# Layer-2 weight conversion, weight sums and pair operands moved from GpSimd to VectorE, and all first-layer casts to ScalarE, in a spectral MLP kernel

## The chip, the core and the metric

The kernel runs on one core of a Trainium2 chip. Its engines are TensorE (PE, matrix products; PEld is its weight load), VectorE (DVE), ScalarE (ACT), GpSimd (POOL) and SyncE (SP), which issues DMAs. The metric is the device time of one execution in microseconds; a kernel's time is the median of several runs.

## What is computed

```python
X = rfft(x, axis=1)                                  # x: (2, 3008, 256)
Yr = Xr @ w_r - Xi @ w_i + b_r;  Yi = Xr @ w_i + Xi @ w_r + b_i
Y = soft-threshold of both by 0.01
x = irfft(Y).reshape(6016, 256)
h = x @ w_in1;  g = max(h, 0) + alpha * min(h, 0);   x = g @ w_out1    # layer 1, 2048 wide
h = x @ w_in2;  g = h if h >= 1, 0 if h <= -1, else (h + 1)**2 / 4     # layer 2, 2048 wide
out = g @ w_out2
```

Every product of the two layers is made of three matmuls: each operand is split into a high part in fp32r (a rounding cast, `gh`, `mxh`, `xo[0]`) and a low part (the fp32 value less its high part, `gl`, `mxl`, `xo[1]`), and low x high, high x low and high x high are added up in PSUM.

## The kernel before

**Stages.** A Fourier stage fills the first 190 us or so. Layer 1 works on 12 chunks of columns, five of 512 and one of 448 for each of the two batches, and 16 blocks `f` of 128 hidden units: 192 steps. The first three chunks are interleaved ("the trio"), and the other nine follow one after the other. One step is `first` (6 matmuls into `psh`, then `ta` and `tb` on ScalarE, a scalar_tensor_tensor on VectorE that joins them into `ta`, then the split of `ta` into `gh` and `gl`) and `second` of the step three back (6 matmuls from `gh`, `gl` into `pso`). `ta` and `tb` have two buffers each, `gh` and `gl` four, `psh` two to four banks. So `ta` of a step waits until `gl` of the step two back has been taken out of the same buffer.

Layer 2 works on six column groups ("pairs", four of 2 x 512 columns and two of 2 x 480) with 8 `quad`s each, 48 in all. A quad makes a 2 x 2 block product from 7 products M1 to M7 in place of 8; it needs sums of the weights (`sum_weights`, three closures for each of the 8 quads of a pair) and sums of the inputs (`prep_pair`, eight stages for each pair). Its 24 output matmuls (`pq`) come one quad later, in four groups.

**Order.** The order of every engine's queue is that in which the code is written; nothing reorders it. Work that isn't part of the step is put in by generators and lists of closures: `conv` (the weight conversion from 64-bit words, pieces of it taken by `next(conv)`), `jobs` and `events`.

**What the change touches.** In the trio, the cast `gh <- ta` is on ScalarE and is written one step later, behind `ta` and `tb` of the next step (`split_late`); in chunks 3 to 11 it is on VectorE at once (`late_split`, L462 to L492). The conversion of layer 1's weights has `conversions(0, ..., V)` and is cut into four pieces for each weight; that of layer 2's weights has `conversions(1, order1, G)`, two pieces for each weight, and its clamp (L194), product (L176), low part (L182) and sum (L183) are on GpSimd. So are the sums L602 to L616 and the differences L643 to L665 of `sum_weights` and `prep_pair`; their high parts (L615, L642) are ScalarE casts. The first pair's operands and the first three weight sums are made during layer 1, are written to DRAM (`keep`) and come back near its end (`fetch`).

Of the kernel before, what the change touches and what calls it, by code (L numbers as in the profile page):

```python
# [89 lines left out]
def spectral_mlp_kernel(ctx: ExitStack, tc: tile.TileContext, x, w_r, w_i, bias, c_f1, c_f2,  # L90
# [483 lines left out]
    X_TAGS = ["c1", "w5", "w6", "w7", "w8", "w9", "w10", "p5", "c2", "c3"]  # L574
    S_TAGS = ["w4", "w11", "w12", "w0", "w1", "w2", "p3", "p4"]
# [17 lines left out]
    def sum_weights(l, j):  # L593
# [3 lines left out]
        def whole():  # L597
            t = block("p0" if j < 3 else "c0", [128, 2, 512], F32, f"sfr{l}_{j}")
            held.extend((t[:, 0, :], t[:, 1, :]))
            for i in range(2):  # L600
                w = wt[l, 2 * j + i]
                G.tensor_tensor(held[0][:, 256 * i:256 * i + 256], w[:, 0, 0:256].bitcast(F32),  # L602
                                w[:, 1, 0:256].bitcast(F32), op=ALU.add)

        def add():
            f4, r4 = (t.rearrange("p (k m) -> p k m", k=4) for t in held)
            G.tensor_tensor(r4[:, 0], f4[:, 2], f4[:, 3], op=ALU.add)
            G.tensor_tensor(r4[:, 2], f4[:, 0], f4[:, 2], op=ALU.subtract)
# [12 lines left out]

        return whole, add, cut

    def prep_pair(p):
# [3 lines left out]
        held = []  # L628
# [4 lines left out]
        def operand(name, v):  # L633
# [130 lines left out]
    def quad(l, p, j, prev, extra, last=False):  # L764
# [21 lines left out]
        A.activation(s5, ps["C"], AF.Copy)  # L786
        if prev:
# [58 lines left out]
    def fetch_w15():  # L846
        wt[1, 15] = fetch(10, "w3", "w1_15k")
# [4 lines left out]
    def fetch_x(k):  # L852
# [3 lines left out]
    ahead = {1: [lambda: fetch_x(0)], 4: [fetch_w15], 5: [lambda: fetch_s(0)], 12: [lambda: fetch_s(1)],  # L856
             13: [lambda: fetch_s(2)]} | {5 + k: [lambda k=k: fetch_x(k)] for k in range(1, 7)}
# [87 lines left out]
```

## Time and profile before

| | us |
|---|---|
| median of 3 runs | 1140.19 (1139.62 to 1140.55) |
| profiled execution | 1139.39 |
| its span from the first to the last instruction | 1137.5 |
| PE busy | 1115.3 (98%) |
| DVE busy | 944.4 (83%) |
| ACT busy | 725.2 (64%) |
| POOL busy | 224.9 (20%) |

Busy time of PE alone does not tell whether it runs at its pace: its matmuls are pipelined, each is shown longer than the distance to the next, so a PE that starts its matmuls late can still look busy. The pace is read from the distance between starts, or from the time that a step or a quad takes. The granted clock is 1.00 in nearly every stretch, which is the upper one of its two levels.

### The profile page before, as it was taken

The page shows a single profiled execution, that of the slowest core. Times are in us where ns is not written, and L with a number is a line of the kernel's source. Part 1 is how long each engine was busy: PE and PEld are TensorE (multiplying, and loading weights), DVE is VectorE, ACT ScalarE, POOL GpSimd, SP SyncE. Part 2 cuts the span into 40 slices and gives each one's busy share as a digit, 9 for nine tenths or more (in the row PEclk, how much of TensorE's full clock was granted, in tenths as well). Part 3 has the DMA queues.
Part 4 walks back from the last instruction along what each step waited for, and adds up shares of the span by engine and source line. Part 5 has one row for each costly group of instructions (what it writes and reads, how often), then busy time and mean ns, then how long its engine had stood idle before and what let it go on. Part 6 is the DMA issues. An engine that isn't in the chain of part 4 may idle for free.

```text
span 1137.5 us, 17421 instructions
## 1 busy us (share of the span) xinstructions
PE 1115.3 (98%) x6488; PEld 983.2 (86%) x6488; DVE 944.4 (83%) x1446; ACT 725.2 (64%) x1356; POOL 224.9 (20%) x190
## 2 busy tenths in 40 slices
PE   9999999999999889999999999999999999999998
PEld 7999988888887877778788997888899888888997
DVE  3689878866689999999999879987887888878876
ACT  3555677866555554545554456676777867767776
POOL 0000000000033535452322114420310402203100
PEclk9999999999999999999999999999999999999999
DMA  9996771010011211111100420010000000000100
GB/s 303 319 310 191 201 155 51 20 56 1 2 56 56 79 52 56 38 37 38 38 1 1 132 73 1 1 38 1 1 38 1 10 27 1 38 1 1 38 1 35
DMA packets 41651, 70.92 MB, mean 62 GB/s; under 512 B 4096, under 2 KB 26464, under 8 KB 41568
## 3 DMA queue, kind: packets, MB, share of 16 engines
q1 hardware_dynamic: 41312, 69.66, 19.3%
q8 instruction: 51, 0.84, 0.3%
q14 instruction: 32, 0.26, 0.1%
q10 hardware_dynamic: 256, 0.16, 0.0%
HBM read 45.30 MB, written 24.51 MB: 61 GB/s over the span
## 4 chain that ended last, share of the span: by engine, by line
PE 75%; DVE 21%; issue 2%; ACT 1%; DVEq 0%; ACTq 0%
DVE ta L490 6%; PE pq L110 6%; PE pq L111 6%; PE pq L109 6%; PE psm L372 6%; DVE gl L106 5%; PE pso L110 4%; PE pso L109 4%; PE psh L109 4%; PE psh L111 4%; PE psh L110 4%; PE pso L111 4%; DVE gh L105 4%; PE ps L292 2%; PE seeded L109 2%; PE seeded L111 2%
## 5 line engine op out<-in xcount | busy, mean ns | idle before, releaser
L487 ACT ACTIVATE ta<-psh 128x512 f32<-128x512 f32 (+1 forms) x192 | 113.5, 591 | 212.5 <-DVE gl L106 147.0
L726 DVE TENSOR_TENSOR gl<-t,gh 128x512 fp32r<-128x512 f32 (+1 forms) x192 | 140.0, 731 | 70.9 <-ACT gh L720 68.1
L490 DVE SCALAR_TENSOR_TENSOR ta<-ta,nalpha,tb 128x512 f32<-128x512 f32 (+1 forms) x192 | 173.3, 902 | 20.7 <-ACT tb L488 20.5
L106 DVE TENSOR_TENSOR gl<-ta,gh 128x512 fp32r<-128x512 f32 (+1 forms) x192 | 150.7, 785 | 35.2 <-ACT gh L103 30.3
L110 PE MATMUL pso<-gl,w 128*128 128x512 f32 (+1 forms) x384 | 146.9, 382 | 10.8 <-DVE gl L106 10.4
L720 ACT ACTIVATE gh<-t 128x512 fp32r<-128x512 f32 (+1 forms) x145 | 89.7, 618 | 98.5 <-DVE t L714 98.3
L109 PE MATMUL pso<-gh,w 128*128 128x512 f32 (+1 forms) x384 | 145.6, 379 | 3.8 <-DVE gh L105 3.8
L109 PE MATMUL psh<-mxh,w 128*128 128x512 f32 (+1 forms) x384 | 144.7, 377 | 0.0
L110 PE MATMUL psh<-mxl,w 128*128 128x512 f32 (+1 forms) x384 | 144.3, 376 | 0.0
L111 PE MATMUL psh<-mxh,w 128*128 128x512 f32 (+1 forms) x384 | 144.3, 376 | 0.0
L111 PE MATMUL pso<-gh,w 128*128 128x512 f32 (+1 forms) x384 | 144.1, 375 | 0.0
L110 PE MATMUL pq<-gl,w 128*128 128x512 f32 (+1 forms) x360 | 136.0, 378 | 2.3 <-DVE gl L726 2.1
L111 PE MATMUL pq<-gh,w 128*128 128x512 f32 (+1 forms) x360 | 134.9, 375 | 0.0
L109 PE MATMUL pq<-gh,w 128*128 128x512 f32 (+1 forms) x360 | 134.9, 375 | 0.0
L488 ACT ACTIVATE tb<-psh 128x512 f32<-128x512 f32 (+1 forms) x192 | 113.0, 589 | 0.0
L110 PEld LDWEIGHTS pso<-gl,w 128*128 128x128 f32 x384 | 72.8, 190 | 28.2 <-DVE gl L106 20.1
L105 DVE CAST gh<-ta 128x512 fp32r<-128x512 f32 (+1 forms) x144 | 76.4, 531 | 15.5 <-DVE ta L490 0.9
L109 PEld LDWEIGHTS pso<-gh,w 128*128 128x128 f32 x384 | 72.8, 190 | 16.0 <-DVE gh L105 7.3
L109 PEld LDWEIGHTS psh<-mxh,w 128*128 128x128 f32 x384 | 72.7, 189 | 9.1 <-ACT tb L488 0.5
L110 PEld LDWEIGHTS pq<-gl,w 128*128 128x128 f32 x360 | 68.0, 189 | 14.3 <-DVE gl L726 6.4
L111 PEld LDWEIGHTS psh<-mxh,w 128*128 128x128 f32 x384 | 72.9, 190 | 8.7
L110 PEld LDWEIGHTS psh<-mxl,w 128*128 128x128 f32 x384 | 72.7, 189 | 8.7
(143 smaller groups left out, 2340.9 us busy)
## 6 DMA issues: line engine op xcount, KB each, us to landing
u<-in_w_in SPq DMA_DIRECT2D x32, 256.0 KB, 3.1
u<-in_w_out SPq DMA_DIRECT2D x32, 256.0 KB, 3.6
v_dr<-ve SPq DMA_DIRECT2D x12, 512.0 KB, 3.9
v<-v_dr SPq DMA_DIRECT2D x32, 192.0 KB, 4.8
x<-in_x SPq DMA_DIRECT2D x15, 384.0 KB, 7.6
out<-yt SPq DMA_DIRECT2D x16, 256.0 KB, 2.2
a_dr<-ae SPq DMA_DIRECT2D x20, 192.0 KB, 6.1
a<-a_dr SPq DMA_DIRECT2D x4, 768.0 KB, 6.3
```

Of the source, the lines that this page charges most:

```text
L105: V.tensor_copy(hi, src)
L106: V.tensor_tensor(lo, src, hi.bitcast(F32), op=ALU.subtract)
L109: T.matmul(ps, wl, xh, start=start, stop=False, skip_group_check=chained)
L110: T.matmul(ps, wh, xl, start=False, stop=False, skip_group_check=chained)
L111: T.matmul(ps, wh, xh, start=False, stop=stop, skip_group_check=chained)
L292: T.matmul(ps[:, u, :], c47, xs[g][:, 2 * i + u, :], start=True, stop=True)
L372: T.matmul(o, x[:, 2 * k + c, off:off + 128], wm[r][:, z, c, :].rearrange("p (h q) -> p q h", h=2), start=n == c == 0, stop=n == 5 and c == 1)
L487: A.activation(ta, ps, AF.Relu, scale=-1.0)
L488: A.activation(tb, ps, AF.Relu)
L490: V.scalar_tensor_tensor(ta, ta, nalpha[:, f:f + 1], tb, op0=ALU.mult, op1=ALU.add)
L720: A.activation(hi, v, AF.Copy)
L726: engine.tensor_tensor(halves(self.gl, self.m), like_halves(self.t, self.m), halves(self.gh, self.m).bitcast(F32), op=ALU.subtract)
```

## The change

The change leaves GpSimd without work. Its operations go to VectorE, written in the same code with `V` in place of `G`. The weight conversion of layer 2 takes the four-piece form, and 9 pieces instead of 4 are taken in each of the chunks 3 to 10. The cut of an operand into high and low part is divided: the ScalarE cast stands at the end of one closure and the VectorE subtraction at the head of the next. The sums for quads 3 to 5 of layer 2 are made in layer 1's last chunk instead of in layer 2's first quads. In every first-layer step the cast `gh <- ta` goes to ScalarE, one step later, as in the trio. Buffers and fetches are moved to suit.

```diff
-    def late_split(step):
-        return step[1] < 3
     def split_late(step):
-        if step is not None and late_split(step):
+        if step is not None:
             split_g(step, A)
...
         V.scalar_tensor_tensor(ta, ta, nalpha[:, f:f + 1], tb, op0=ALU.mult, op1=ALU.add)
-        if not late_split((l, c, f)):
-            split_g((l, c, f), V)
...
-                G.tensor_tensor(held[0][:, 256 * i:256 * i + 256], w[:, 0, 0:256].bitcast(F32),
+                V.tensor_tensor(held[0][:, 256 * i:256 * i + 256], w[:, 0, 0:256].bitcast(F32),
                                 w[:, 1, 0:256].bitcast(F32), op=ALU.add)
         def add():
-            G.tensor_tensor(r4[:, 0], f4[:, 2], f4[:, 3], op=ALU.add)
+            V.tensor_tensor(r4[:, 0], f4[:, 2], f4[:, 3], op=ALU.add)
...
+        def high():
+            A.activation(s[:, 0, :], held[1], AF.Copy)
         def cut():
-            A.activation(s[:, 0, :], r, AF.Copy)
-            G.tensor_tensor(s[:, 1, :], r, s[:, 0, :].bitcast(F32), op=ALU.subtract)
+            V.tensor_tensor(s[:, 1, :], held[1], s[:, 0, :].bitcast(F32), op=ALU.subtract)
...
             A.activation(hi, v, AF.Copy)
-            G.tensor_tensor(lo, v, hi.bitcast(F32), op=ALU.subtract)
+            def cut():
+                V.tensor_tensor(lo, v, hi.bitcast(F32), op=ALU.subtract)
...
+at(1, lambda: fetch_x(0))
+for k in range(1, 7):
+    at(9 + k, lambda k=k: fetch_x(k))
+for j in range(3):
+    at(13 + j, lambda j=j: fetch_s(j))
+for j in range(3, 6):
+    for k in range(4):
+        at(2 + 4 * (j - 3) + k, SUM[j][k])
...
-            conv = conversions(1, order1, G)
+            conv = conversions(1, order1, V)
...
-        if 5 <= i < len(trio) and i % 8 != 0 or l == 0 and c >= 3 and (f % 4 == 0 or f == 13 and 5 <= c < 9):
+        if 5 <= i < len(trio) and i % 8 != 0 or l == 0 and c >= 3 and (f % 2 == 0 or f == 13):
             next(conv, None)
-        if 4 <= c < NC - 1 and f % 4 == 2:
+        if 4 <= c < NC - 1 and (f % 4 == 3 or f % 4 == 1 and f > 8 and 6 <= c < 8):
             next(jobs, lambda: None)()
...
-    for k, g in enumerate([g for j in range(3, NJ) for g in SUM[j]]):
-        events[(0, k // 3, k % 3)] = g
+    for at_k, g in zip(((0, 0, 0), (0, 0, 1), (0, 0, 2), (0, 1, 0), (0, 1, 1), (0, 1, 2), (0, 2, 0), (0, 2, 1)), SUM[6] + SUM[7]):
+        events[at_k] = g
     for p in range(1, len(pairs1)):
-        for (j, k), g in zip(((5, 0), (5, 1), (5, 2), (6, 1), (7, 0), (7, 1), (8, 0), (8, 1)), prep_pair(p)):
+        for (j, k), g in zip(((4, 1), (5, 1), (6, 1), (7, 0), (7, 1), (7, 2), (8, 0), (8, 1)), prep_pair(p)):
```

What the queues then hold is shown at three places. VectorE in layer 1, chunk 6, steps 8 and 9, before (`ta`, `gh`, `gl` are the step's own, `mxl` prepares the next chunk, `cm` belongs to a weight's conversion):

```order
L106 TENSOR_TENSOR mxl_7_4815<-yt_3232,mxh_7_4814 128x1024
L490 SCALAR_TENSOR_TENSOR ta_6_8_4833<-ta_6_8_4833,nalpha,tb_6_8_4834 128x512
L105 CAST gh_6_8_4831<-ta_6_8_4833 128x512
L106 TENSOR_TENSOR gl_6_8_4832<-ta_6_8_4833,gh_6_8_4831 128x512
L170 SCALAR_TENSOR_TENSOR cm_5_4733<-cm_5_4733,cp_5_4734 128x512
L490 SCALAR_TENSOR_TENSOR ta_6_9_4858<-ta_6_9_4858,nalpha,tb_6_9_4859 128x512
L105 CAST gh_6_9_4856<-ta_6_9_4858 128x512
L106 TENSOR_TENSOR gl_6_9_4857<-ta_6_9_4858,gh_6_9_4856 128x512
```

and now:

```order
L106 TENSOR_TENSOR mxl_7_4828<-yt_3233,mxh_7_4827 128x1024
L106 TENSOR_TENSOR gl_6_7_4815<-ta_6_7_4816,gh_6_7_4814 128x512
L487 SCALAR_TENSOR_TENSOR ta_6_8_4846<-ta_6_8_4846,nalpha,tb_6_8_4847 128x512
L182 TENSOR_TENSOR cm_5_4568<-cm_5_4568,w_5_4796 128x512
L183 TENSOR_TENSOR w_5_4796<-cm_5_4568,cp_5_4569 128x512
L106 TENSOR_TENSOR gl_6_8_4845<-ta_6_8_4846,gh_6_8_4844 128x512
L487 SCALAR_TENSOR_TENSOR ta_6_9_4870<-ta_6_9_4870,nalpha,tb_6_9_4871 128x512
L106 TENSOR_TENSOR gl_6_9_4869<-ta_6_9_4870,gh_6_9_4868 128x512
```

The cast is gone from VectorE, `gl` stands ahead of the next step's join, and the conversion's L182 and L183 have come in from GpSimd.

ScalarE at the same place, before:

```order
L103 ACTIVATE mxh_7_4814<-yt_3232 128x1024
L487 ACTIVATE ta_6_8_4833<-psh_6_8_4824 128x512
L488 ACTIVATE tb_6_8_4834<-psh_6_8_4824 128x512
L487 ACTIVATE ta_6_9_4858<-psh_6_9_4849 128x512
L488 ACTIVATE tb_6_9_4859<-psh_6_9_4849 128x512
```

and now:

```order
L103 ACTIVATE mxh_7_4827<-yt_3233 128x1024
L484 ACTIVATE ta_6_8_4846<-psh_6_8_4837 128x512
L485 ACTIVATE tb_6_8_4847<-psh_6_8_4837 128x512
L103 ACTIVATE gh_6_7_4814<-ta_6_7_4816 128x512
L484 ACTIVATE ta_6_9_4870<-psh_6_9_4861 128x512
L485 ACTIVATE tb_6_9_4871<-psh_6_9_4861 128x512
L103 ACTIVATE gh_6_8_4844<-ta_6_8_4846 128x512
```

Each step has a third ScalarE instruction, the cast of the step before.

VectorE in layer 2, at the head of quad 7 of the first pair (`t` and `gl` belong to a block's activation and its low part, `h` is a block's input, `xo` an operand of the next pair, `xt` its temporary), before:

```order
L714 SCALAR_TENSOR_TENSOR t_0_13_0_7665<-t_0_13_0_7665,seeded_7003 128x512
L726 TENSOR_TENSOR gl_0_13_0_7706<-t_0_13_0_7665,gh_0_13_0_7703 128x512
L812 TENSOR_TENSOR h_0_14_1_7660<-psC_0_7_7657,s_1_0_7_7659 128x512
L813 TENSOR_TENSOR h_0_15_1_7661<-seeded_7086,s_1_0_7_7658 128x512
L714 SCALAR_TENSOR_TENSOR t_0_14_0_7700<-t_0_14_0_7700,psA_0_7_7656 128x512
```

and now:

```order
L721 SCALAR_TENSOR_TENSOR t_0_13_0_7663<-t_0_13_0_7663,seeded_7029 128x512
L641 TENSOR_TENSOR xoB_1_7612<-yt_1302,xoB_1_7612 128x512
L667 TENSOR_TENSOR xt_7427<-yt_1302,xt_7427 128x512
L733 TENSOR_TENSOR gl_0_13_0_7704<-t_0_13_0_7663,gh_0_13_0_7701 128x512
L641 TENSOR_TENSOR xoT_1_7684<-xt_7427,xoT_1_7684 128x512
L672 TENSOR_TENSOR xt_7427<-yt_1302 128x512
L821 TENSOR_TENSOR h_0_14_1_7658<-psC_0_7_7655,s_1_0_7_7657 128x512
L822 TENSOR_TENSOR h_0_15_1_7659<-seeded_7115,s_1_0_7_7656 128x512
L721 SCALAR_TENSOR_TENSOR t_0_14_0_7698<-t_0_14_0_7698,psA_0_7_7654 128x512
```

Four operand instructions stand ahead of `h` and of the join that reads `psA`; one more comes later in this quad and two at the head of the next.

## Rows read from the trace of the kernel before

**Rows 1.** Busy time of engines in five stretches; the first line names the columns.

```profile
core 0: us, PE busy (x) PEld busy (x) DVE busy (x) ACT busy (x) POOL busy (x), PEclk, DMA share, GB/s
190.00:300.00 110.00, 110.00 (x747) 96.22 (x746) 81.39 (x129) 78.37 (x144) 0.86 (x1) 1.00 0.08 25
345.00:562.00 217.00, 202.33 (x911) 170.78 (x910) 206.25 (x267) 115.26 (x210) 97.55 (x77) 0.99 0.15 52
672.30:714.30 42.00, 40.58 (x182) 33.36 (x181) 38.79 (x53) 28.77 (x54) 22.26 (x28) 1.00 0.00 1
773.40:802.60 29.20, 29.20 (x138) 25.55 (x137) 22.55 (x40) 20.40 (x37) 0.00 (x0) 1.00 0.00 1
```

**Rows 2.** Waits, 345 to 562 us: waiter, releaser, us in total, times, longest.

```profile
ACT ta L487 <- DVE gl L106: 95.1, 52, 3.6
PE pso L110 <- DVE gl L106: 10.4, 18, 1.2
```

**Rows 3.** VectorE groups, 190 to 300 us: xcount, busy us, mean ns, idle before.

```profile
L490 DVE SCALAR_TENSOR_TENSOR ta<-ta,nalpha,tb 128x512 f32<-128x512 f32 x42 | 31.4, 747 | 4.9 <-ACT tb L488 4.7
L106 DVE TENSOR_TENSOR gl<-ta,gh 128x512 fp32r<-128x512 f32 x43 | 29.7, 691 | 20.8 <-ACT gh L103 20.5
L105 DVE CAST gh<-ta 128x512 fp32r<-128x512 f32 x10 | 4.5, 449 | 1.4 <-DVE ta L490 0.5
L176 DVE TENSOR_TENSOR cp<-cp,u 128x512 f32<-128x512 f32 x5 | 4.3, 863 | 0.2
L106 DVE TENSOR_TENSOR mxl<-yt,mxh 128x1024 fp32r<-128x1024 f32 x2 | 2.4, 1218 | 0.0
```

**Rows 4.** VectorE groups, 345 to 562 us.

```profile
L490 DVE SCALAR_TENSOR_TENSOR ta<-ta,nalpha,tb 128x512 f32<-128x512 f32 x60 | 63.4, 1056 | 0.0
L106 DVE TENSOR_TENSOR gl<-ta,gh 128x512 fp32r<-128x512 f32 x59 | 52.1, 883 | 2.0
L105 DVE CAST gh<-ta 128x512 fp32r<-128x512 f32 x60 | 32.6, 544 | 6.2
L490 DVE SCALAR_TENSOR_TENSOR ta<-ta,nalpha,tb 128x448 f32<-128x448 f32 x16 | 17.1, 1066 | 0.0
```

**Rows 5.** ScalarE in the trio, in order of time: start, duration, idle and its releaser.

```profile
200.95 0.60 ACT L487 ACTIVATE ta<-psh 128x512 f32<-128x512 f32 x1
201.92 0.63 ACT L103 ACTIVATE gh<-ta 128x512 fp32r<-128x512 f32 x1
...
203.72 0.64 ACT L487 ACTIVATE ta<-psh 128x512 f32<-128x512 f32 x1
...
206.17 0.60 ACT L487 ACTIVATE ta<-psh 128x512 f32<-128x512 f32 x1 [0.82 <-DVE gl L106]
...
208.77 0.60 ACT L487 ACTIVATE ta<-psh 128x512 f32<-128x512 f32 x1 [0.99 <-DVE gl L106]
```

**Rows 6.** The same view, later in the trio.

```profile
246.60 0.60 ACT L487 ACTIVATE ta<-psh 128x512 f32<-128x512 f32 x1 [0.96 <-PE psh L111]
...
249.19 0.60 ACT L487 ACTIVATE ta<-psh 128x512 f32<-128x512 f32 x1 [0.99 <-PE psh L111]
...
254.37 0.60 ACT L487 ACTIVATE ta<-psh 128x512 f32<-128x512 f32 x1 [0.99 <-PE psh L111]
...
257.76 0.61 ACT L487 ACTIVATE ta<-psh 128x512 f32<-128x512 f32 x1
```

**Rows 7.** VectorE in a quad of the second pair, in order of time.

```profile
773.44 0.69 DVE L812 TENSOR_TENSOR h<-psC,s 128x512 f32<-128x512 f32 x1
...
774.70 0.68 DVE L714 SCALAR_TENSOR_TENSOR t<-t,psA 128x512 f32<-128x512 f32 x1
...
782.42 0.69 DVE L726 TENSOR_TENSOR gl<-t,gh 128x512 fp32r<-128x512 f32 x1 [1.36 <-ACT gh L720]
783.15 0.69 DVE L812 TENSOR_TENSOR h<-psC,s 128x512 f32<-128x512 f32 x1
```

**Rows 8.** TensorE in the same quad: the first matmul of the next quad's M1.

```profile
777.12 0.38 PE L109 MATMUL psA<-xoB,w 128*128 128x512 f32 x1
```

**Rows 9.** VectorE group in the first four quads, 672.3 to 714.3 us.

```profile
L726 DVE TENSOR_TENSOR gl<-t,gh 128x512 fp32r<-128x512 f32 x16 | 16.0, 1017 | 3.1 <-ACT gh L720 3.0
```

More of the change, by code (lines that the diff above doesn't have):

```diff
@@ L606, in add @@
             f4, r4 = (t.rearrange("p (k m) -> p k m", k=4) for t in held)
-            G.tensor_tensor(r4[:, 0], f4[:, 2], f4[:, 3], op=ALU.add)
-            G.tensor_tensor(r4[:, 2], f4[:, 0], f4[:, 2], op=ALU.subtract)
-            G.tensor_tensor(r4[:, 1], r4[:, 0], f4[:, 0], op=ALU.subtract)
-            G.tensor_tensor(r4[:, 3], f4[:, 1], r4[:, 1], op=ALU.subtract)
+            V.tensor_tensor(r4[:, 0], f4[:, 2], f4[:, 3], op=ALU.add)
+            V.tensor_tensor(r4[:, 2], f4[:, 0], f4[:, 2], op=ALU.subtract)
+            V.tensor_tensor(r4[:, 1], r4[:, 0], f4[:, 0], op=ALU.subtract)
+            V.tensor_tensor(r4[:, 3], f4[:, 1], r4[:, 1], op=ALU.subtract)
+        def high():
+            s = kept_tile(f"sk{l}_{j}") if j < 3 else block(S_TAGS[j], [128, 2, 512], F32R, f"s{l}_{j}")
+            sums[l, j] = s
+            A.activation(s[:, 0, :], held[1], AF.Copy)
         def cut():
-            r = held[1]
-            s = kept_tile(f"sk{l}_{j}") if j < 3 else block(S_TAGS[j], [128, 2, 512], F32R, f"s{l}_{j}")
-            A.activation(s[:, 0, :], r, AF.Copy)
-            G.tensor_tensor(s[:, 1, :], r, s[:, 0, :].bitcast(F32), op=ALU.subtract)
+            s = sums[l, j]
+            V.tensor_tensor(s[:, 1, :], held[1], s[:, 0, :].bitcast(F32), op=ALU.subtract)
             if j < 3:
                 keep(7 + j, s)
-            else:
-                sums[l, j] = s
-        return whole, add, cut
+        return whole, add, high, cut
     def prep_pair(p):
@@ L642, in operand, with cut @@
             A.activation(hi, v, AF.Copy)
-            G.tensor_tensor(lo, v, hi.bitcast(F32), op=ALU.subtract)
-            if p == 0:
-                keep(k, t)
+            def cut():
+                V.tensor_tensor(lo, v, hi.bitcast(F32), op=ALU.subtract)
+                if p == 0:
+                    keep(k, t)
+            cuts.append(cut)
+        def cut():
+            cuts.pop(0)()
         def stage0():
@@ L649, in stage0 @@
             held.extend(tmp[:, z, :m] for z in range(2))
-            G.tensor_tensor(held[0], src(0, 1), src(0, 0), op=ALU.subtract)
+            V.tensor_tensor(held[0], src(0, 1), src(0, 0), op=ALU.subtract)
+            operand("B11", src(0, 0))
         def stage1():
-            operand("B11", src(0, 0))
-            G.tensor_tensor(held[1], src(1, 1), held[0], op=ALU.subtract)
+            cut()
+            V.tensor_tensor(held[1], src(1, 1), held[0], op=ALU.subtract)
+            operand("T1", held[0])
         def stage2():
-            operand("T1", held[0])
+            cut()
+            operand("B21", src(1, 0))
         def stage3():
-            operand("B21", src(1, 0))
-            G.tensor_tensor(held[0], src(1, 0), held[1], op=ALU.subtract)
+            cut()
+            V.tensor_tensor(held[0], src(1, 0), held[1], op=ALU.subtract)
+            operand("T2", held[1])
         def stage4():
-            operand("T2", held[1])
-            G.tensor_tensor(held[1], src(1, 1), src(0, 1), op=ALU.subtract)
+            cut()
+            V.tensor_tensor(held[1], src(1, 1), src(0, 1), op=ALU.subtract)
+            operand("B22", src(1, 1))
         def stage5():
-            operand("B22", src(1, 1))
+            cut()
+            operand("T3", held[1])
         def stage6():
-            operand("T3", held[1])
-        def stage7():
+            cut()
             operand("T4", held[0])
-        return stage0, stage1, stage2, stage3, stage4, stage5, stage6, stage7
+        return stage0, stage1, stage2, stage3, stage4, stage5, stage6, cut
     def product(l, name, ps, p, j, start):
@@ L786, in quad @@
         A.activation(s5, ps["C"], AF.Copy)
+        if not prev:
+            split_late(seq[-1])
         if prev:
@@ L846, in fetch_w15 @@
     def fetch_w15():
-        wt[1, 15] = fetch(10, "w3", "w1_15k")
+        wt[1, 15] = fetch(10, "p3", "w1_15k")
     def fetch_s(j):
@@ L854, in fetch_x, with at @@
         xop[0][name] = fetch(k, X_TAGS[k], f"xo{name}_0")
-    ahead = {1: [lambda: fetch_x(0)], 4: [fetch_w15], 5: [lambda: fetch_s(0)], 12: [lambda: fetch_s(1)],
-             13: [lambda: fetch_s(2)]} | {5 + k: [lambda k=k: fetch_x(k)] for k in range(1, 7)}
+    ahead = {}
+    def at(f, g):
+        ahead.setdefault(f, []).append(g)
+    at(1, lambda: fetch_x(0))
[6 more added lines that the diff above has]
+            at(2 + 4 * (j - 3) + k, SUM[j][k])
     for i in range(len(seq)):
@@ L889, in spectral_mlp_kernel @@
     events = {}
-    for k, g in enumerate([g for j in range(3, NJ) for g in SUM[j]]):
-        events[(0, k // 3, k % 3)] = g
+    for at_k, g in zip(((0, 0, 0), (0, 0, 1), (0, 0, 2), (0, 1, 0), (0, 1, 1), (0, 1, 2), (0, 2, 0), (0, 2, 1)), SUM[6] + SUM[7]):
+        events[at_k] = g
     for p in range(1, len(pairs1)):
-        for (j, k), g in zip(((5, 0), (5, 1), (5, 2), (6, 1), (7, 0), (7, 1), (8, 0), (8, 1)), prep_pair(p)):
+        for (j, k), g in zip(((4, 1), (5, 1), (6, 1), (7, 0), (7, 1), (7, 2), (8, 0), (8, 1)), prep_pair(p)):
             events[(p, 0, k) if j == NJ else (p - 1, j, k)] = g
+    late = events[0, 0, 2]
+    events[0, 0, 2] = lambda: (late(), fetch_w15())
     prev = None
```

6 lines of the change are left out of this document (3 added, 3 removed).

## The prediction

> **What bounds the kernel now.** I read the busy times by stretch first. In the trio (190 to 300 us) TensorE is busy without a pause; from 345 to 562 us it is not, and there VectorE is busy 206.25 of 217 us and GpSimd 97.55 [rows 1]. The waits of that stretch give the chain: ScalarE's `ta` waits 95.1 us for the low part `gl`, whose buffer it reuses, and TensorE's `pso` matmuls wait for the same `gl` [rows 2]. So VectorE paces layer 1 there. How much that costs is not in the wait rows, since a pipelined matmul that starts late still looks busy. I take it from the pace. When TensorE alone sets it, two `ta` that wait for `psh` stand 2.59 us apart (246.60 to 249.19) [rows 6]; a step of 448 columns, by the ratio of columns, takes 2.27. The stretch holds 60 joins of 512 and 16 of 448 columns [rows 4]: 60 x 2.59 + 16 x 2.27 = 191.7 us of work in 217 us, **25.3 us lost**. Why VectorE is late is seen from one instruction in two stretches: the join L490 takes 747 ns in the trio [rows 3], where GpSimd did 0.86 us of work, and 1056 ns beside it [rows 4]; `gl` 691 and 883, the cast 449 and 544. Layer 2 shows the same in its first quads: four take 42.0 us with GpSimd at 22.26, where three quiet ones take 29.2 [rows 1], and `gl` takes 1017 ns [rows 9]. 42.0 - 4 x 9.73 = 3.1 us; GpSimd's sums go on over about one quad more, so I take **4 us lost**. In the quiet quads TensorE has no pause.
>
> **Layer 1, VectorE's load.** For the same 76 steps: 206.25 us now. The casts leave: 60 x 0.544 and 16 no dearer, together 41. The stretching beside GpSimd leaves: joins 60 x (1.056 - 0.747) = 18.5 and 16 x (1.066 - 0.65) = 6.6, low parts 59 x (0.883 - 0.691) = 11.3 [rows 3, 4]; 36 in all. The conversion comes in: 76 steps hold 4.75 chunks of 9 pieces, 10.7 weights of four instructions (0.863 for the product [rows 3], two at 0.69 like `gl`, a clamp no dearer than that): 2.9 us each, 31. The first pair's 11 operand instructions at 0.69 are 8. Three weight sums have 6 pieces of 256, 12 of 128 and 3 of 512 columns. No row shows two-input pieces so short; each costs between its share of the columns of 0.69 (0.35 and 0.17) and the whole 0.69, in sum between 6 and 14. I take what the nearest two rows give: 1024 columns take 1218 ns and 512 take 691 [rows 3], so 1.03 ns a column and 0.16 us once, 0.43 and 0.30, in sum 8. Sum: 206 - 41 - 36 + 31 + 8 + 8 = 176 of 191.7 us. VectorE is then 92% loaded (95% at the upper bound) and no longer the bound by load.
>
> **Layer 1, the loop.** ScalarE gets one cast of 0.63 us [rows 5] for each step: 115.26 + 76 x 0.63 = 163 of 191.7 us. On VectorE the same cast is the shorter, 0.449 us [rows 3], but there it would lie on the fuller queue: 176 + 76 x 0.449 = 210 us, 18 more than TensorE needs. The Trainium skill, ScalarE: Activation LUTs, section Rules for kernel authors, tells to use VectorE and not ScalarE for simple elementwise work because it is faster per element; the trace agrees on the durations, and by that rule the step would stay bound by VectorE and lose some 18 us, where this change is forecast to lose 2.5. Load is not all, because the cast closes a loop: `ta` and `tb` of a step, the cast of the step before, its `gl` on VectorE, and only then `ta` again. The trio already runs this loop with conversion pieces on VectorE in most steps, so its rows are prices for the new one. From `ta` to `ta`: 2.77 us with two conversion instructions on ScalarE, 2.45 with one small one on VectorE, 2.60 with the two long ones on VectorE [rows 5]. The fourth kind of piece has two VectorE instructions too, one of them short; at 2.45 to 2.60 the mean of the four is 2.57 to 2.6, the pace of TensorE. A step without a piece is no dearer than 2.45 and gains back 0.14. What a chunk adds beside: the two evictions and the preparation of the next chunk, which together made one step 3.39 (254.37 to 257.76) [rows 6], 0.8 too long; and at f = 7 a preparation with a pair or sum stage on VectorE, 0.69 + 0.75 + 1.22 + up to 2 x 0.69 = 4.0 [rows 3], 1.4 too long. A chunk with all of this (4 to 7) falls behind by about 0.8 + 1.4 less 7 x 0.14 = 1.2 us; chunks 8 to 10 have no such stage and catch up. `second` comes three steps after `first`, and `gl` is due before then by about one step: I estimate that 2.5 us of lateness are hidden. Four chunks at 1.2 are 4.8 us, so some **2.5 us stay lost**; bounds 0 and 9 chunks x 1.2 = 11. In the last chunk the sums for quads 3 to 5 meet steps whose conversion is done: at nothing, covered by the missing pieces; the upper end is inside the 11.
>
> **Layer 2.** In a quiet quad VectorE has (29.20 - 22.55) / 3 = 2.2 us free [rows 1]. In the first three quads only sums 6 and 7 are made, 5.5 us by the prices above (4 to 10), into 6.65 us free, and nothing is stretched. The 4 us come back but for 0.5. At a pair's end it is tighter. The 11 operand instructions go to five quads; four stand at the head of quad 7. Two of them lie in a gap of 1.36 us before `gl` [rows 7], at nothing. Two (1.26 us, as from 773.44 to 774.70 two such instructions take) stand ahead of `h` and the join of `psA`. That join ends at 774.70 + 0.68 = 775.38, and the next M1, which writes `psA`, starts at 777.12 [rows 7, 8]: 1.74 us are free, 0.4 stay. The three that follow add 0.65 each, less what the gap takes: 2.0 to 2.5 of lateness against 1.74, about 0.5 us for each of the five pair changes, **2.5 us**; bounds 0 and 1.5 each (all five of the last instructions on the path less 1.74), 7.5. What GpSimd's overlap costs there today is not counted as a gain.
>
> **DMA.** SP issues the same transfers in another order. Each fetch into layer 1's last chunk waits for the last use of a layer-1 weight, and the latest of them (sum 0, into the buffer of f = 9) is due three steps after that, some 7 us. Price nothing; if it were late, quad 0 would wait a few microseconds once, inside the range.
>
> **Sum.** Against the profiled execution: 1139.39 - 25.3 + 2.5 - 4 + 0.5 + 2.5 = 1115.6. The median lies 0.8 us above that execution, so **1116 us**, bounds 1139.4 - 29.3 = 1110 and 1139.4 - 29.3 + 11 + 7.5 + 0.5 = 1129.
>
> **The rivals.** *Bunches:* VectorE stays the pacemaker where pieces meet: every chunk loses 1.2 and every pair change 1.5. For it: 92% load leaves little to catch up with. Against: the trio, 747 matmuls with no pause [rows 1]. 1129 us. *The cast loop, slower:* the cast of a step waits behind what VectorE does before its join, so every step with a piece costs 2.77 and every step with a stage or sum 0.8 too much: 72 x 0.18 + 32 x 0.8 = 38.6 us lost in place of 29.3, with the pair ends' 2.5 some 12 us slower: 1151 us. It decides from a mean excess of 29.3 / 144 = 0.2 us a step. Against: 206.17 and 208.77 lie 2.60 apart with the two longest pieces [rows 5]. *It does not do what it says:* the stretching comes from VectorE's own pace of waits and not from GpSimd; then the load is 206 - 41 + 47 = 212 us and the time stays, 1140 us. Against: the two-input instructions are at 690 to 750 ns in the trio, where GpSimd is idle [rows 1, 3].
>
> **How the numbers follow.** Forecast 70% (1110 to 1121), bunches 20% (1121 to 1129), the slower loop 6%, no effect 4%. A measurement tells about 0.2%, 2.3 us, from no change. Faster 0.90, same 0.04, slower 0.06. The range 1110 to 1128 takes in the forecast and most of the bunches; the last two, 10%, and a little on either side are left out.
>
> **What would show it.** Right: the join back at 0.75 us and `gl` at 0.69 in layer 1; 16 steps of 2.59 in chunks 8 to 10 with `ta` waiting for `psh`; small waits near f = 7 of chunks 4 to 7; the first quads at 9.7 us; at pair changes `psA` waiting for the join by half a microsecond. Wrong: `ta` waiting for `gl` in most steps of layer 1 at a distance over 2.6, TensorE's waits in quads 7 and 0 of over 1.5 us for each pair, ScalarE or VectorE waiting for a DMA, or a granted clock that falls where TensorE no longer pauses (it is 1.00, the upper level, in the trio [rows 1]).

## The result and the profile after

| | before | after |
|---|---|---|
| median, us | 1140.37 (1139.62 to 1141.38, 4 runs) | 1112.12 (1111.45 to 1113.41, 4 runs) |
| profiled execution, us | 1139.39 | 1111.69 |
| ratio of the times | | 0.9753, 95% interval 0.9736 to 0.977 |

The change saves 28 us; 1116 us was forecast, in a range of 1110 to 1128. The page of the changed kernel, its first lines on span and engines, and the first line of the chain that ended last, followed by the same line of the kernel before:

```profile
span 1109.9 us, 17210 instructions
PE 1104.5 (100%) x6488; PEld 985.4 (89%) x6488; DVE 871.2 (78%) x1488; ACT 795.3 (72%) x1500; POOL 0.2 (0%) x4
...
PE 98%; ACT 1%; DVE 0%; issue 0%; ACTq 0%
```

```profile
PE 75%; DVE 21%; issue 2%; ACT 1%; DVEq 0%; ACTq 0%
```

The chain now runs along TensorE nearly from end to end, where a fifth of it ran along VectorE. VectorE got GpSimd's work and is busy for less time than before (871 us against 944): the casts that left it and the stretching that ended weigh more than what came in.

The busy times by stretch (columns as in [rows 1]; 200 us of layer 1 from step f = 9 of chunk 4 to f = 7 of chunk 9, and the first quads of layer 2):

```profile
345.00:545.00 200.00, 199.97 (x950) 178.92 (x949) 163.68 (x273) 158.57 (x294) 0.00 (x0) 1.00 0.16 55
...
648.00:690.00 42.00, 41.80 (x195) 36.38 (x194) 36.47 (x68) 29.58 (x57) 0.00 (x0) 1.00 0.00 1
```

The trio takes 123.3 us as it did, from its first `ta` to that of chunk 3. The 217 us of [rows 1] held 76 steps, and these 200 us hold 80 (64 and 16 joins). Chunks 4 to 8, from the first `ta` of chunk 4 to that of chunk 9, took 229.0 us and now take 203.9, and TensorE pauses in them for 0.4 us only. In the first quads 42 us hold 195 matmuls where they held 182. The VectorE groups of 345 to 545 us, which answer [rows 4] (xcount, busy us, mean ns, idle before), and the waits of 345 to 562 us, which answer [rows 2] (us in total, times, longest):

```profile
L487 DVE SCALAR_TENSOR_TENSOR ta<-ta,nalpha,tb 128x512 f32<-128x512 f32 x64 | 47.8, 747 | 0.0
L106 DVE TENSOR_TENSOR gl<-ta,gh 128x512 fp32r<-128x512 f32 x64 | 44.2, 691 | 29.0 <-ACT gh L103 28.6
```

```profile
ACT ta L484 <- DVE gl L106: 40.8, 50, 1.7
DVE gl L106 <- ACT gh L103: 37.3, 42, 2.0
...
PEld pso L110 <- DVE gl L106: 0.7, 2, 0.4
```

The join is back at 747 ns and `gl` at 691. `ta` still waits for `gl`, for 40.8 us in place of 95.1, but next to nothing that TensorE needs is late by it: its own wait for `gl` is 0.7 us. That `ta` waits for `gl` is harmless as long as `second`, which comes three steps later, still finds its `gl` ready.

### The profile page after: what moved, and what is told of

Read it like the earlier page. It is cut to its first block, busy times and chain, and to the rows that moved or that the text cites. A ratio compares the mean times of both kernels' runs of the same rounds, so it can differ in the third digit from the quotient of the medians.

```text
span 1109.9 us, 17210 instructions
## 1 busy us (share of the span) xinstructions
PE 1104.5 (100%) x6488; PEld 985.4 (89%) x6488; DVE 871.2 (78%) x1488; ACT 795.3 (72%) x1500; POOL 0.2 (0%) x4
## 4 chain that ended last, share of the span: by engine, by line
PE 98%; ACT 1%; DVE 0%; issue 0%; ACTq 0%
PE pso L109 7%; PE pso L110 7%; PE psh L109 7%; PE psh L111 7%; PE psh L110 7%; PE pso L111 7%; PE pq L110 7%; PE pq L111 7%; PE pq L109 7%; PE psm L372 6%; PE seeded L111 3%; PE seeded L110 3%; PE seeded L109 3%; PE ps L292 3%; PE psA L109 2%; PE psf L352 2%
## 5 line engine op out<-in xcount | busy, mean ns | idle before, releaser
L106 DVE TENSOR_TENSOR gl<-ta,gh 128x512 fp32r<-128x512 f32 (+1 forms) x192 | 130.7, 681 | 121.7 <-ACT gh L103 120.7
L733 DVE TENSOR_TENSOR gl<-t,gh 128x512 fp32r<-128x512 f32 (+1 forms) x192 | 130.4, 679 | 67.2 <-ACT gh L727 64.3
L110 PE MATMUL pso<-gl,w 128*128 128x512 f32 (+1 forms) x384 | 144.1, 375 | 0.0
L487 DVE SCALAR_TENSOR_TENSOR ta<-ta,nalpha,tb 128x512 f32<-128x512 f32 (+1 forms) x192 | 141.3, 736 | 0.0
L103 ACT ACTIVATE gh<-ta 128x512 fp32r<-128x512 f32 (+1 forms) x192 | 120.2, 626 | 0.0
L109 PEld LDWEIGHTS pso<-gh,w 128*128 128x128 f32 x384 | 72.6, 189 | 8.7
L111 PEld LDWEIGHTS pso<-gh,w 128*128 128x128 f32 x384 | 72.6, 189 | 8.5
```

The source lines that it names most:

```text
L103: A.activation(hi, src, AF.Copy)
L106: V.tensor_tensor(lo, src, hi.bitcast(F32), op=ALU.subtract)
L109: T.matmul(ps, wl, xh, start=start, stop=False, skip_group_check=chained)
L110: T.matmul(ps, wh, xl, start=False, stop=False, skip_group_check=chained)
L111: T.matmul(ps, wh, xh, start=False, stop=stop, skip_group_check=chained)
L733: engine.tensor_tensor(halves(self.gl, self.m), like_halves(self.t, self.m), halves(self.gh, self.m).bitcast(F32), op=ALU.subtract)
```

## The experiments

Each was timed together with the kernel before (1140.09 to 1140.59 us). "Over after" is the difference to 1112.12. The traces below are shown from 345 to 545 us where nothing else is said; a slower kernel gets through fewer steps in these 200 us.

| run | us | ratio to before, 95% interval | over after, us |
|---|---|---|---|
| e1_casts_back | 1121.32 | 0.9834 [0.9817, 0.985] | +9.2 |
| e2_casts_only | 1142.9 | 1.0026 [1.0017, 1.0036] | +30.8 |
| e3_gpsimd_load | 1127.51 | 0.989 [0.9875, 0.9904] | +15.4 |
| e3b_gpsimd_paced | 1155.25 | 1.013 [1.0115, 1.0145] | +43.1 |
| e4a_act_outside | 1113.93 | 0.9771 [0.9754, 0.9787] | +1.8 |
| e4b_act_inside | 1123.45 | 0.9853 [0.9838, 0.9867] | +11.3 |
| e5_big_pieces | 1129.78 | 0.9912 [0.9898, 0.9927] | +17.7 |
| e6_sums_on_gpsimd | 1121.57 | 0.9837 [0.9822, 0.9852] | +9.4 |
| e7_cast_behind_copy | 1112.31 | 0.9756 [0.974, 0.9773] | +0.2 |
| e8_conversion_on_gpsimd | 1124.88 | 0.9866 [0.9852, 0.9881] | +12.8 |

### The two halves of the change: e1 and e2

**e1** is the changed kernel with the casts of chunks 3 to 11 back on VectorE:

```diff
+    def late_split(step):
+        return step[1] < 3
-        if step is not None:
+        if step is not None and late_split(step):
...
+        if not late_split((l, c, f)):
+            split_g((l, c, f), V)
```

> Changed kernel with the casts of chunks 3 to 11 back on VectorE; GpSimd stays empty. If VectorE's load matters: 76 steps need 176 + 76 x 0.45 = 210 us of VectorE against 191.7 of TensorE, about 0.24 us late per step, over the 128 steps of chunks 3 to 10 up to 30 us, less where chunks 8 to 10 have no stages: 1128 to 1140 us. If only GpSimd's overlap mattered: 1112 to 1115 us.

**e2** is the reverse: the kernel before with these casts on ScalarE one step later, and GpSimd keeps its work.

> Kernel before with only the casts moved to ScalarE one step later; GpSimd keeps its work. If VectorE's load in busy time decides: 206 - 41 = 165 us of 191.7, layer 1 is back at TensorE's pace and only the 4 us of the first quads stay: 1114 to 1119 us. If the loop through ta, tb, the cast and gl decides: each step beside GpSimd has a gl or join stretched by about 0.9 us, 2.42 + 0.9 = 3.3 us, and with GpSimd busy 45% of the time the mean step is about 2.8: 0.2 us late over 128 steps, 1130 to 1142 us.

Measured, 1121.3 and 1142.9 us: e1 below its range of 1128 to 1140, e2 just above 1130 to 1142. The 200 us of e1 (window, the join, the cast, the wait of `ta`):

```profile
345.00:545.00 200.00, 196.79 (x905) 168.37 (x904) 188.50 (x333) 114.43 (x204) 0.00 (x0) 1.00 0.16 56
```

```profile
L490 DVE SCALAR_TENSOR_TENSOR ta<-ta,nalpha,tb 128x512 f32<-128x512 f32 x59 | 43.9, 744 | 0.0
L105 DVE CAST gh<-ta 128x512 fp32r<-128x512 f32 x59 | 25.2, 427 | 6.1
```

```profile
ACT ta L487 <- DVE gl L106: 77.0, 60, 2.6
```

and of e2:

```profile
345.00:545.00 200.00, 186.58 (x841) 155.38 (x840) 141.69 (x177) 145.13 (x264) 84.78 (x72) 1.00 0.14 51
```

```profile
L487 DVE SCALAR_TENSOR_TENSOR ta<-ta,nalpha,tb 128x512 f32<-128x512 f32 x54 | 55.0, 1018 | 0.0
L106 DVE TENSOR_TENSOR gl<-ta,gh 128x512 fp32r<-128x512 f32 x54 | 42.5, 786 | 45.8 <-ACT gh L103 45.7
```

```profile
DVE gl L106 <- ACT gh L103: 58.2, 64, 1.5
ACT ta L484 <- DVE gl L106: 42.1, 49, 2.2
PE pso L110 <- DVE gl L106: 11.6, 25, 1.6
```

Four times make a square: before 1140, casts alone 1143, all but the casts 1121, both 1112. "All but the casts" is GpSimd emptied together with the smaller conversion pieces and the new places of the sums, which e5, e6 and e8 take apart in part. It is worth 19 us with the casts on VectorE and 31 with them on ScalarE; moving the casts is worth 9 us in its company and *costs* 2.8 without it. The gain is no sum of two parts.

e2 shows why load is not the whole story. VectorE is busy 141.69 of 200 us there, less than in any other version, and TensorE gets through 841 matmuls in place of 950. Its joins are stretched to 1018 ns, and the loop `ta`, `tb`, join, cast, `gl` passes two of VectorE's instructions and three of ScalarE's in turn, whoever is idle between them.

In e1 VectorE is nearly full (188.5 of 200 us busy) and `ta` waits for `gl` twice as long (77.0 us for 38.6). That the load decides there is read from these numbers; no run separates it from the place of the cast in the loop. e1 came 7 us below its lowest expectation, which had added durations. On this engine neighbours overlap: over 345 to 545 us the durations of VectorE's instructions add up to about 201 us in e1 and 180 in the changed kernel, where the windows show 188.5 and 163.7 busy.

e1 also weighs a rule. The cast of 512 columns takes 427 ns on VectorE in e1 and 636 on ScalarE in the changed kernel, and with the slower instruction the kernel is 9.2 us faster. VectorE is the fuller queue of the two. The Trainium skill, ScalarE: Activation LUTs, section Rules for kernel authors, tells to use VectorE and not ScalarE for `relu`, `max`, `min`, `add` and `mul`, as faster per element; a cast isn't in its list. Carried over to this cast, the durations agree with it, the time does not.

### GpSimd beside VectorE: e3, e3b, e6, e8

**e3** adds GpSimd work that nothing needs to the changed kernel, 165 us of it where the change takes 225 away:

```diff
+        if 3 <= c < NC - 1:
+            for _ in range(2):
+                G.tensor_tensor(scratch, b_t[:, 0, 0:128], b_t[:, 0, 128:256], op=ALU.add)
```

> Changed kernel with two GpSimd additions of 128 columns in each step of chunks 3 to 10, from a constant tile into a scratch tile that nobody reads, so that nothing waits for them. If GpSimd's overlap stretches VectorE: about 0.45 us of VectorE per us of GpSimd (48 of 97.55 in the stretch before), 0.5 us per step, and joins or gl of over 1 us where they meet: 1135 to 1160 us. If the stretching had another cause: 1112 to 1113 us and joins at 0.75 us.

Measured, 1127.5 us, +15.4, below the expected 1135 to 1160. It didn't load the stage it was meant for: the additions wait for nothing but their constant, so all 256 ran in the Fourier stage and the trio, before layer 1's later chunks began. GpSimd's group in e3, and then the 200 us of layer 1:

```profile
L892 POOL TENSOR_TENSOR scratch<-b_t 128x128 f32<-128x128 f32 x256 | 165.2, 645 | 53.8 <-DMA b_t<-in_bias 33.8
```

```profile
345.00:545.00 200.00, 200.00 (x951) 179.11 (x950) 163.66 (x272) 159.28 (x296) 0.00 (x0) 1.00 0.16 56
```

This is still a test, in the other stage. Three VectorE groups of the stretch from 60 to 215 us, first in e3, then in the changed kernel:

```profile
L379 DVE TENSOR_TENSOR y<-t,clip 128x512 f32<-128x512 f32 x19 | 15.8, 831 | 0.7
L377 DVE TENSOR_TENSOR t<-psm,b_t 128x512 f32<-128x512 f32 x19 | 12.8, 676 | 1.2 <-PE psm L372 1.2
L194 DVE TENSOR_SCALAR cm<-cm 128x512 f32<-128x512 f32 x12 | 8.1, 677 | 0.0
```

```profile
L379 DVE TENSOR_TENSOR y<-t,clip 128x512 f32<-128x512 f32 x19 | 13.2, 693 | 0.7
L377 DVE TENSOR_TENSOR t<-psm,b_t 128x512 f32<-128x512 f32 x19 | 13.0, 683 | 2.5 <-PE psm L372 2.3
L194 DVE TENSOR_SCALAR cm<-cm 128x512 f32<-128x512 f32 x14 | 5.9, 421 | 0.0
```

Same operation, same shape: the one with both operands in SBUF goes from 693 to 831 ns beside GpSimd, the one with an operand in PSUM (`psm`) stays at 676 to 683. Two inputs are not needed for it, though: the clamp L194 has one input, in SBUF, and goes from 421 to 677 ns. The Trainium skill, GPSIMD Engine Reference, section Specifications, says that GpSimd shares its SBUF interfaces with VectorE and names as contending the instructions with two SBUF inputs and those in a 2-port performance mode. The first two groups agree; in which mode L194 ran, no row shows.

**e3b** paces the same kind of work with layer 1 by letting it read the `gh` just made:

```diff
+            g = gt[before][0].bitcast(F32)
...
+                G.tensor_tensor(scratch, g[:, 0:180], g[:, 256:436], op=ALU.add)
```

> As e3, but the two GpSimd additions (180 columns each) read the high part that the step has just made, so they run beside layer 1 and not at the start; nobody reads their result. If GpSimd's reads stretch VectorE: 48 us of stretch for some 33 thousand GpSimd columns in the kernel before, 1.45 ns a column, 0.5 us a step, of which gl's third lies in the loop: 0.15 us over 128 steps less what is hidden, 1118 to 1132 us, with joins at 0.85 to 1.0 us. If not: 1112 us.

Measured, 1155.3 us, +43.1 and slower than the kernel before: the size is a miss, by 23 us over the upper end. The 200 us of e3b:

```profile
345.00:545.00 200.00, 179.10 (x804) 147.85 (x803) 183.99 (x236) 136.73 (x251) 122.41 (x134) 1.00 0.15 53
```

```profile
L492 POOL TENSOR_TENSOR scratch<-gh 128x180 f32<-128x180 f32 x134 | 123.0, 918 | 77.6 <-ACT gh L103 72.4
L493 DVE SCALAR_TENSOR_TENSOR ta<-ta,nalpha,tb 128x512 f32<-128x512 f32 x51 | 52.0, 1019 | 0.0
L106 DVE TENSOR_TENSOR gl<-ta,gh 128x512 fp32r<-128x512 f32 x52 | 45.1, 868 | 11.6 <-ACT gh L103 11.3
```

The additions start when the cast ends, which is when `gl` starts and the next join follows: the means of VectorE's two instructions in the loop rise by 0.27 and 0.18 us. But it is mostly the amount that is larger: GpSimd is busy for 236 us in chunks 3 to 11 here, for 85 in e8 and 56 in e6 (both below), and each of these microseconds costs TensorE 0.18 us of pauses in layer 1 here, 0.15 in e8 and in e6 (42.5, 13.0 and 8.5 us of pauses more than in the changed kernel). Whether the place in the step adds to that isn't shown; no run moved the same additions to another place of the step.

**e6** puts the weight sums and pair operands of the changed kernel back on GpSimd, **e8** the conversion's product, low part, sum and clamp; all else stays in its place.

```diff
 e6, eleven times in sum_weights and prep_pair
-            V.tensor_tensor(...)
+            G.tensor_tensor(...)
 e8, with the four pieces for each weight kept
-            conv = conversions(1, order1, V)
+            conv = conversions(1, order1, G)
```

> Changed kernel with the weight sums and pair operands back on GpSimd at the new places; conversion on VectorE and casts on ScalarE. If all work beside VectorE costs by its stretch: layer 2's pair changes lose about 0.3 us each as before and layer 1's steps with such a stage up to 1 us each, most of it hidden: 1114 to 1122 us. If the conversion alone was the trouble: 1111 to 1113 us.

> The changed kernel with the four instructions of layer 2's conversion that it took from GpSimd (product, low part, sum and clamp of each weight) given back to GpSimd; their places in the code, the sums and operands on VectorE and the casts on ScalarE stay. In the kernel before these instructions were 91 us of GpSimd, nearly all in layer 1. Theory 'stretch': beside GpSimd the two-input instructions of VectorE take longer, joins and low parts of the loop among them; the sums and operands, 28 us of GpSimd in layer 1, cost 6.9 us there, so 91 us cost about 22, in which VectorE's lighter queue (some 40 us of conversion gone from it) gives a part back: 1122 to 1134 us, joins of 0.9 us and more in layer 1. Theory 'load': what counts is how much VectorE has to do; with 40 us less the changed kernel's small residual in layer 1 goes as well: 1110 to 1113 us.

Measured, 1121.6 (the upper end) and 1124.9 us. Window and join, of e6 and then of e8:

```profile
345.00:545.00 200.00, 195.94 (x918) 171.40 (x917) 159.72 (x236) 154.52 (x286) 28.43 (x28) 1.00 0.15 53
```

```profile
L487 DVE SCALAR_TENSOR_TENSOR ta<-ta,nalpha,tb 128x512 f32<-128x512 f32 x61 | 51.2, 840 | 0.0
```

```profile
345.00:545.00 200.00, 194.72 (x896) 167.85 (x896) 148.82 (x214) 149.49 (x275) 59.75 (x44) 0.99 0.16 56
```

```profile
L484 DVE SCALAR_TENSOR_TENSOR ta<-ta,nalpha,tb 128x512 f32<-128x512 f32 x58 | 49.7, 856 | 0.0
```

In both, VectorE has less to do than in the changed kernel (236 and 214 instructions in the stretch against 273, 159.7 and 148.8 us busy against 163.7) and TensorE gets less done (918 and 896 matmuls against 950). Fewer steps in the stretch are a part of that, but over the whole execution VectorE is also busy for less time, 863.0 and 861.3 us against 871.2. So the theory that only VectorE's load counts falls; what GpSimd takes off VectorE's list it takes back with more by stretching what is left in the loop. +9.4 and +12.8 make +22, where e2, with both on GpSimd and the old larger pieces, has +30.8.

### Where an instruction stands in the loop: e4a and e4b

The same ScalarE instruction is added to every step of chunks 3 to 10: in e4a behind the cast, in e4b between `tb` and the cast.

```diff
             split_late(before)
+            A.activation(scratch, b_t[:, 0, 0:128], AF.Copy)   # e4a; e4b: ahead of split_late
```

> Changed kernel with one ScalarE copy of 128 columns (0.28 us) from a constant tile into a scratch tile in each step of chunks 3 to 10, written behind the cast. If the loop decides: it lies in the 0.75 us that ScalarE waits for gl, and costs only in the steps where conversion, eviction or preparation fill that gap, about a quarter: 1113 to 1118 us. If ScalarE's load decides, the same as for the next one.

> The same instruction in the same steps, but written between tb and the cast. If the loop decides, the whole 0.28 us lengthens each turn: 2.42 becomes 2.70, 112 steps of chunks 4 to 10 lose up to 0.28 each less 0 to 5 us that they get back now: 1135 to 1143 us. If only ScalarE's load counts (159 of 200 us busy), its idle time takes it: 1112 to 1118 us, as for the one before.

Measured, +1.8 and +11.3 us, for 0.32 us of ScalarE in each step of either. The instruction and the waits of 345 to 545 us, of e4a and then of e4b:

```profile
L490 ACT ACTIVATE scratch<-b_t 128x128 f32<-128x128 f32 x78 | 25.0, 320 | 0.0
```

```profile
ACT ta L486 <- DVE gl L106: 28.2, 43, 1.3
```

```profile
L489 ACT ACTIVATE scratch<-b_t 128x128 f32<-128x128 f32 x75 | 23.5, 313 | 0.0
```

```profile
ACT ta L486 <- PE psh L111: 19.7, 25, 0.8
PEld pso L110 <- DVE gl L106: 17.4, 68, 0.9
```

Outside the loop it falls into the time in which ScalarE waits for `gl` anyway (38.6 us in that stretch of the changed kernel, 28.2 left here), and overlaps its neighbours. Inside, TensorE waits for `gl` 68 times. So the loop of latency (`ta`, `tb`, cast, `gl`, and `ta` again, each waiting for the one before) is real, and there is little room in it. The size is a miss, 1123 for an expected 1135 or more. Eight chunks of 16 steps at 0.31 us would be 40 us; it is 11, so nearly three quarters of what is put into the loop is hidden; in which steps, these rows don't tell.

### The size of the pieces: e5

The conversion in two pieces for each weight, as before, instead of four; all of it on VectorE.

```diff
-                if E is V:
+                if l == 0:
...
-... and (f % 2 == 0 or f == 13)
+... and (f % 4 == 0 or f == 13 and 5 <= c < 9)
```

> Changed kernel with layer 2's conversion in two pieces for each weight in place of four, at the step numbers of the kernel before, all on VectorE. If load decides, the work is the same: 1112 to 1114 us. If the loop decides: each weight has one step with about 2.3 us of ScalarE pieces (0.75 fit) and one with 2.5 us of VectorE pieces (1.2 fit), some 2.8 us late in two steps, and gets back 0.17 in each of five others: 1.9 us for each of 16 weights, less 2.5 hidden: 1130 to 1142 us.

Measured, 1129.8 us, +17.7, just under the expected 1130 to 1142:

```profile
345.00:545.00 200.00, 190.72 (x874) 162.66 (x873) 155.01 (x257) 146.15 (x272) 0.00 (x0) 1.00 0.16 56
```

```profile
ACT ta L484 <- DVE gl L106: 53.1, 53, 2.7
PE pso L110 <- DVE gl L106: 8.7, 19, 1.5
```

GpSimd is empty here, joins are not stretched (745 ns) and the instructions are the same; VectorE is busy 155 of 200 us, far from full, and TensorE waits. What differs is how much work comes in a row between two turns of the loop, and in how many steps. Undoing the small pieces costs more than half of the change's whole gain.

### The pauses at the pair changes: e7

A pair change is the end of a pair's quad 7 with the first quads, 0 and 1, of the next pair. The prediction had put 2.5 us at the pair changes, on a join of VectorE. The trace of the changed kernel has pauses there, but they name another engine. TensorE's waits from 700 to 1100 us, and ScalarE at the head of the second pair:

```profile
PEld psA L109 <- ACT seeded L792: 3.2, 10, 0.4
```

```profile
718.79 1.14 ACT L718 ACTIVATE t<-t 128x512 f32<-128x512 f32 x2
719.83 0.62 ACT L638 ACTIVATE xoT<-xt 128x512 fp32r<-128x512 f32 x1
720.35 0.58 ACT L707 ACTIVATE t<-seeded 128x512 f32<-128x512 f32 x1
720.83 0.59 ACT L792 ACTIVATE seeded<-psA 128x512 f32<-128x512 f32 x1
```

M1 writes `psA`, ScalarE copies it out (L792), and only then M2 may write `psA`. The operand's cast L638 now stands ahead of the copy; at the same place of the kernel before (749.01 to 749.49) L700 and the copy follow the squares at once. Ten waits are two in each of the five pair changes: in quad 0, and in quad 1, where evictions stand ahead of the copy as they did before. In quad 1 it is VectorE that is later. Its queue there, and ScalarE's `gh`, which waits for the join:

```profile
725.71 0.69 DVE L641 TENSOR_TENSOR xoT<-xt,xoT 128x512 fp32r<-128x512 f32 x1
...
727.51 0.68 DVE L721 SCALAR_TENSOR_TENSOR t<-t,psA 128x512 f32<-128x512 f32 x1
```

```profile
728.23 0.64 ACT L727 ACTIVATE gh<-t 128x512 fp32r<-128x512 f32 x1 [1.32 <-DVE t L721]
```

From 728.23 on ScalarE has no gap up to its copy at 730.75. The operand's subtraction L641 stands ahead of the join, which ends 0.50 us before M1 starts (728.70); at the same place of the kernel before it ended 1.19 us before M1, and over the five pair changes it is 0.7 to 1.2 us later than it was. e7 leaves that alone and moves the one ScalarE cast of quad 0 behind the copies:

```diff
-            A.activation(hi, v, AF.Copy)
+            if p > 0 and name == "T3":
+                casts.append(lambda: A.activation(hi, v, AF.Copy))
+            else:
+                A.activation(hi, v, AF.Copy)
...
         A.activation(s5, ps["C"], AF.Copy)
+        while casts:
+            casts.pop(0)()
```

> The changed kernel, with one ScalarE instruction moved: the cast of the operand T3, which stands at the end of quad 7 of each pair but the last, goes behind the two copies (psA to seeded, psC to s) at the head of the next pair's quad 0. In the changed kernel TensorE pauses at the second product into psA (M2) of that quad by 0.11 to 0.30 us, 0.82 us in all in five pair changes, and its weight load names the ScalarE copy as what it waited for. Theory 'ScalarE queue': the cast, 0.6 us, stands ahead of the copy, so those five pauses go (the copy starts about 0.5 us earlier), and the pauses of quad 1, before which nothing moves, stay at some 1.1 us. Rival 'VectorE operands' (the prediction's own): the operand subtractions on VectorE make the join late, so the pauses stay where they are. In time 0.8 us, which three rounds hardly tell: 1111 to 1112.5 against 1112.1; the trace decides.

Measured, 1112.31 us, which can't be told from 1112.12. TensorE's waits of the same stretch in e7:

```profile
PEld psA L109 <- ACT seeded L797: 1.7, 5, 0.3
...
PEld seeded L109 <- ACT s L818: 1.1, 5, 0.3
```

The five waits of quad 0 are gone and those of quad 1 are left: without the cast ahead of the copy quad 0 has no such pause. Its join was not moved, and ScalarE waits for it ahead of the squares, so e7 doesn't show that the join has no part. Five new waits came in, of M7 for the next ScalarE copy (L818), which reads what M6 wrote. By distances between matmul starts, quad 0's pauses at M2 were 0.82 us, and 0.45 us stand at M7 now. ScalarE's queue is full over those microseconds, and the cast's half microsecond moves along it. The pauses of all pair changes add up to 2.0 us, as without e7's move. With this, the changed kernel stays the fastest; its TensorE has some 3 us of pauses left from chunk 4 to the last pair change.

## Why the prediction was right, and where not

Pauses of TensorE are distances between starts of neighbouring matmuls over the usual 0.21 to 0.22 us (0.20 for 480 columns), added up.

**Layer 1: right.** 25.3 us were said to be lost and 2.5 to stay. The join and `gl` went back to 747 and 691 ns, the values of the trio that the prediction took. What stays is 0.4 us, nearly all at one place of chunk 6, where `second` needs the `gl` of f = 7. TensorE there (start, duration):

```profile
424.70 0.38 PE L109 MATMUL pso<-gh,w 128*128 128x512 f32 x1
425.12 0.48 PE L110 MATMUL pso<-gl,w 128*128 128x512 f32 x1
425.44 0.38 PE L111 MATMUL pso<-gh,w 128*128 128x512 f32 x1
```

It is the place that was named, the step behind f = 7 with its preparation and stage, and 0.42 and 0.32 us stand where 0.21 should. The lateness of `ta` behind TensorE rises to 2.5 to 2.8 us before TensorE stops, close to the estimate of 2.5. What was too large is the term of 1.2 us a chunk: from one chunk's first `ta` to the next one's, chunk 4 falls behind by 1.25 us, chunk 5 by 0.9, and chunks 6 and 7 not at all. With TensorE's own pauses that is some 2.3 us where 4.8 were added up. The steps come back to `ta` waiting for `psh` in chunk 9 and not in chunk 8 (from 545 to 620 us, 22 such waits against 3 for `gl`).

**VectorE's load: mis-sized.** 176 us were forecast for 76 steps; 163.68 us for 80 joins make 155. The sum started from a busy time and took off and added durations, as if the overlap of neighbours stayed the same; it rose from 9.5 us (215.7 of durations in 206.25 busy) to 16 (180 in 163.7). It also left out that the 448-column `gl` was stretched (955 ns before, 630 now, 5 us for 16 of them). What makes up the rest of the 21 us was not worked out. It made no difference to the sum of the time, since load was no longer the bound; it made the rival *bunches* look nearer than it was, and it misled e1's expectation.

**The loop: right in kind.** The step's distance was taken to be set by pieces of conversion in a loop of latency. e4b and e5 show the loop and the pieces to matter, e4a that ScalarE's work outside of it hardly does (+1.8 us).

**First quads: right.** 4 us lost were said to leave 0.5. The pauses there were 4.9 us and are 0.5. It takes both parts of the change: in e6 the sums for quads 3 to 5 stand at their new places but on GpSimd, the pauses of the first quads are 1.1 us, and layer 1's last chunk, which holds these sums, takes 37.5 us in place of 34.5.

**Pair changes: near in size, wrong in the path.** Forecast were 2.5 us of new pauses, with M1 waiting for the join of `psA`. That join ends 0.4 to 0.7 us before M1 starts in every pair change, and M1 doesn't wait; M2 does, for ScalarE's copy of what M1 wrote. These new pauses are some 1.9 us: about 1.1 in quad 1, where the operand's subtraction makes the join late, as the prediction said of VectorE, and ScalarE passes that on, and 0.8 in quad 0, where by e7 a ScalarE cast ahead of the copy is needed for them. The part of quad 1 is read from the trace; no run moved the subtraction. The prediction counted VectorE's instructions of the moved stages and not ScalarE's. Before, the pauses there were 1.2 us, nearly all of another kind, TensorE's wait for a `gl` (742 to 1100 us):

```profile
PEld pq L110 <- DVE gl L726: 1.6, 4, 0.5
```

Of these, 0.2 us are left, a gain that the prediction said it doesn't count. So the pair changes hold 2.0 us of pauses in all, 0.8 more than before.

**The sum.** By the starts of `ta` in the two profiled executions, the part from chunk 4 to the last step of layer 1 fell from 345.1 to 319.8 us, so 25.3 were saved; the part behind it fell from 469.5 to 466.2, so 3.3 (4.4 in the first quads, less 0.8 and a few tenths). The part before chunk 4 took 1.0 us longer. The executions differ by 27.7 us; forecast were 23.8. The 1.0 us can't be told from chance: the first `ta` starts anywhere from 146.6 to 148.9 us in the traces of the kernels here that share this stage (all but e3), at 146.6 before and 147.6 after.

**The rivals.** *Bunches* (1129) is the time of e5, with pieces twice as large. *The slower loop* (1151) needs more in the loop than the change puts there; e2 with its stretched joins, at 1143, is the nearest to it. *No effect* falls with e3, e6 and e8: it is GpSimd's work that stretches VectorE's.

## What to carry to other kernels

Work on GpSimd is not free because its queue is off the critical path: ask which VectorE instructions with inputs in SBUF run beside it, and whether they stand in a loop. Where an engine waits though it is far from full, follow the loop of instructions that hands one buffer round, and price what stands in that loop; the same instruction cost 1.8 us outside and 11.3 us inside. When a stage is moved, count what it issues on every engine, since a part of the pauses came from the engine that wasn't counted.

## What the runs showed of the hardware

- VectorE's instructions with both inputs in SBUF take longer beside GpSimd (join 747 to 1018 ns in e2, `y` 693 to 831 in e3); the one with an input in PSUM didn't (683 and 676). Instructions with a single input in SBUF can take longer too: the clamp L194 421 to 677 ns in e3, the cast 449 to 544 [rows 3, 4]. GpSimd work that nobody needed, 165 us of it, cost 15 us of time in e3; 236 us of it beside layer 1 cost 43 in e3b, more than the whole change brought.
- Neighbouring instructions of VectorE overlap: about 180 us of durations are 163.7 us of busy time, and 201 are 188.5 in e1. Sums of durations overstate its load, here by 7 to 10%.
- A pause of TensorE costs a little more than the wait: in the rows above, the matmul that waited (425.12) is shown at 0.48 us in place of 0.38, and the one behind it starts 0.32 us later in place of 0.21. Nearly every pause at a pair change has that 0.1 us behind it too.
